# First pair of heads prepared on three engines, a new order of the attention, and a moved output and a moved turn in the expert stage

## The chip, the cores and the metric

One Trainium2 chip, one of its cores. The metric is the device time of one launch in microseconds (us). A core has five engines with their own instruction queues: PE (matrix multiplication, with its weight loads shown as PEld), DVE (vector), ACT (scalar), POOL (GpSimd) and SP, which here only issues transfers. An engine runs its queue in order.

## The reference, cut to what matters

Three steps, each on the result of the one before: attention with queries averaged in pairs, a dense layer pair with h − tanh(h), and a mixture of eight experts of which each token takes one.

```python
q_pool = q.reshape(B, H, S // 2, 2, D).mean(axis=3)        # B 2, H 8, S 1152, D 64
scores = scale * np.matmul(q_pool, k.transpose(0, 1, 3, 2))
attn = np.exp(scores - scores.max(-1)); attn /= attn.sum(-1) + 1e-9
x = (attn @ v) -> (1152, 512)
h = x @ w_in; x = (h - np.tanh(h)) @ w_out                  # 512 -> 2048 -> 512
logits = x @ w_gate; expert_idx = np.argmax(logits, axis=1) # 8 experts, 288 places each
y = relu(disp[e] @ w1[e]) @ w2[e]                           # 512 -> 1024 -> 512
out[i] = gate_w[i] * y[expert_idx[i], pos[i]]
```

## The kernel before

**Attention.** The 16 heads go in eight pairs. `load_k` (L513), `prep_q` (L547) and L596 load k, q and v of a pair through SP. To multiply in full precision, k and the summed q are split into a high and a low half: `khi` (L461) copies k rounded, `klo` (L470) subtracts it from k; `qadd` (L553) adds the two queries of a pair, `qhi` (twice) and `qlo` split the sum by the same helpers. All of these run on POOL. PE transposes them (`ktr` L534, `qtr` L570), and ACT moves the transposes out of PSUM (`kev`, `qev`, L459). Then a pair has nine units of 128 query rows: PE multiplies (`qk`, L664), DVE takes the maximum (L670), ACT the exponential (L678), POOL splits the result into two 16-bit halves (L689, two instructions a unit; ACT does a few of them, L691), and a transposing DMA from SP (L694) brings it into `pt`, a single buffer for all pairs. Units 3 and 7 of a pair are transposed on PE instead (L706, L720, L723). When the pair's units stand in `pt`, PE multiplies with v in two halves of 72 matmuls (L736; this is the AV phase), and only as its matmuls have read `pt` can the next pair's transposes write there. Behind it the sums are divided out (L800).

**Dense layers.** L906 multiplies with `w_in`, L963 with `w_out`; the weights are loaded during the attention and split by ACT and DVE (L873 to L880).

**Experts.** Rows are scattered to lists by expert; per expert one block of 64 rows always runs. `hidden(e)` (L1389) multiplies with w1, ACT applies relu (L1394), `turn(e)` transposes (four transposes on PE, L1400, into the one PSUM buffer `ht`, and one ACT copy into `hT`, L1404), `project(e)` (L1414, four chunks of w2) multiplies with w2, `output(e)` scales by the gate (ACT L1421, DVE L1424) and scatters to the result (POOL L1270). The gate values come with a small transfer of their own (L1332). The inputs of experts 0 and 1 stand transposed in PSUM first and are copied by `xth0` (L459 on ACT); those of the others are transposed by PE at L1349 and copied by `xth1` to `xth3` (L459 ACT, L460 DVE). Where an expert has more than 64 rows, the others run as its overflow: `over_first` transposes them (L1496), copies them on DVE (L1499), and multiplies with w1 (64 matmuls, L1503, relu on DVE L1506); a second half follows (L1518). With this data experts 0 and 4 have one.

**What sets the order.** A planner (class `Plan`) takes each operation with the buffers it reads and writes, a cost, and a due time `at` (shifted by kind through the table `ORDER`), and writes one order per engine: an operation goes in by due time once what it needs is there by the modelled times. In the expert stage `P.seq` keeps the order by due time alone:

```python
t = at + 9.9 if e == 0 else at + 5.0
over_first(e, t)
project(e, at + 5.6)
output(e, at + 9.2)
```

## Time and profile before

| what | before |
|---|---|
| median of 3 runs | 654.37 us (652.66 to 654.85) |
| the profiled execution | 655.12 us, span 653.1 us |
| TensorE's granted clock, mean | 0.971 |
| PE busy | 588.3 us (90%) |
| DVE, ACT, POOL busy | 373.9, 349.8, 348.0 us (57%, 54%, 53%) |

The span is the time from the first to the last instruction that the profile shows; the launch adds 2.0 us in this execution. Busy time is a sum over stages that have different limits, so a stage is read by itself: who is busy there, and for what the others wait. [...]

### The profile page before, as it was taken

What the parts mean: (1) busy time and instruction counts of PE and PEld (TensorE: products, weight loads), DVE (VectorE), ACT (ScalarE), POOL (GpSimd) and SP (SyncE); (2) the same over time, 40 slices, a digit from 0 to 9 for tenths busy, and PEclk for the clock granted to TensorE, in tenths of its full rate; (3) what the DMA queues carried; (4) which work ended last, traced back from release to release, by engine and by line L of the source; (5) the groups of instructions that cost most, each with busy time, mean ns of one, the idle gap of its engine ahead of it and who ended that gap; (6) DMA issues with size and microseconds to landing.
All of it is one profiled execution on the core that took longest, in us unless ns stands there. A gap on an engine that the chain in (4) does not pass through costs nothing. (4 is left out here: it accounts for less than half of the span.)

```text
span 653.1 us, 10491 instructions
## 1 busy us (share of the span) xinstructions
PE 588.3 (90%) x3840; PEld 471.9 (72%) x3840; DVE 373.9 (57%) x579; ACT 349.8 (54%) x641; POOL 348.0 (53%) x303
## 2 busy tenths in 40 slices
PE   3879898979898979999999999899999959999993
PEld 2767787867786868888899999799989456338331
DVE  1687767695777686898879896854554021101100
ACT  4886877776868786856775766544441100120011
POOL 7996959696969588976446365522232100110111
PEclk9979999998999999999999999899998979999997
DMA  7799989998999695999935123344277843595000
GB/s 217 167 200 204 218 195 204 219 212 172 192 214 211 128 176 124 162 349 356 411 131 178 34 67 95 119 139 129 67 215 249 224 128 129 178 371 190 22 24 13
DMA packets 172371, 114.82 MB, mean 176 GB/s; under 512 B 135470, under 2 KB 144686, under 8 KB 172048
## 3 DMA queue, kind: packets, MB, share of 16 engines
q1 hardware_dynamic: 169152, 109.37, 64.5%
q0 software_dynamic: 1680, 3.81, 1.9%
q10 hardware_dynamic: 1472, 0.79, 0.6%
q8 instruction: 37, 0.61, 0.4%
q14 instruction: 30, 0.25, 0.1%
HBM read 66.22 MB, written 16.15 MB: 126 GB/s over the span
## 5 line engine op out<-in xcount | busy, mean ns | idle before, releaser
L470 POOL TENSOR_TENSOR b<-b,b 128x512 fp32r<-128x512 f32 (+2 forms) x88 | 149.9, 1715 | 97.8 <-ACT b L459 80.6
L689 POOL TENSOR_SCALAR b<-b 128x1152 f16<-128x1152 uint16 (+1 forms) x110 | 131.5, 1216 | 42.1 <-ACT b L678 37.8
L963 PE MATMUL psum<-b,b 128*128 128x512 f32 x432 | 118.3, 400 | 4.3 <-POOL b L470 3.7
L670 DVE CUSTOM_DVE_ANT_1 b<-psum,na 128x1152 f16<-128x1152 f32 x72 | 97.5, 1355 | 42.5 <-PE psum L664 34.8
L906 PE MATMUL psum<-b,b 128*128 128x384 f32 x576 | 116.0, 340 | 1.0 <-DVE b L723 1.0
L906 PEld LDWEIGHTS psum<-b,b 128*128 128x128 f32 x576 | 103.8, 190 | 8.3 <-DVE b L723 1.3
L678 ACT ACTIVATE b<-psum,b 128x1152 int32<-128x1152 f32 (+1 forms) x72 | 88.0, 1222 | 39.3 <-DVE b L670 36.2
L664 PE MATMUL psum<-b,b 128*128 128x384 f32 x384 | 87.5, 365 | 18.0 <-ACT b L678 17.3
L963 PEld LDWEIGHTS psum<-b,b 128*128 128x128 f32 x432 | 79.5, 189 | 17.9 <-POOL b L470 5.4
L664 PEld LDWEIGHTS psum<-b,b 128*128 128x128 f32 x384 | 67.3, 197 | 26.6 <-ACT b L678 21.5
L459 ACT ACTIVATE b<-psum 128x384 fp32r<-128x384 f32 (+3 forms) x119 | 60.2, 540 | 46.1 <-PE psum L963 14.6
L736 PE MATMUL psum<-b,b 128*64 128x288 f16 x1152 | 81.1, 293 | 3.7 <-DMA b<-b 1.4
L736 PEld LDWEIGHTS <-b 128*64 128x64 f16 x1152 | 64.9, 112 | 15.7 <-issue 10.4
L459 ACT ACTIVATE b<-b 128x512 fp32r<-128x512 f32 (+1 forms) x56 | 39.7, 720 | 48.3 <-DVE b L937 25.8
L1270 POOL DMA_INDIRECT out_dram<-b,b x8 | 7.3, 916 | 80.2 <-DVE b L1424 40.2
L1424 DVE SCALAR_TENSOR_TENSOR b<-psum,b,b 64x512 f32<-64x512 f32 x8 | 5.9, 742 | 70.1 <-ACT b L1421 70.1
L1404 ACT ACTIVATE b<-psum 128x512 f32<-128x512 f32 x8 | 4.8, 597 | 58.6 <-PE psum L1400 58.6
L878 DVE SCALAR_TENSOR_TENSOR b<-b,b 128x512 uint32<-128x512 uint32 x32 | 34.7, 1101 | 0.2
L929 DVE SCALAR_TENSOR_TENSOR b<-psum,b 128x768 f32<-128x768 f32 x24 | 22.8, 952 | 17.3 <-ACT b L924 8.2
L880 DVE SCALAR_TENSOR_TENSOR b<-b,b 128x512 uint32<-128x512 uint32 x32 | 32.4, 1026 | 0.2
L1389 PE MATMUL psum<-b,b 128*64 128x512 f32 x128 | 30.6, 602 | 2.0 <-ACT b L459 1.4
L723 DVE SCALAR_TENSOR_TENSOR b<-psum,b 128x384 f16<-128x384 f32 x48 | 25.0, 551 | 12.1 <-ACT b L720 12.1
(130 smaller groups left out, 803.2 us busy)
## 6 DMA issues: line engine op xcount, KB each, us to landing
b<-in_moe_w_dram SPq DMA_DIRECT2D x64, 512.0 KB, 6.0
b<-in_moe_w_in_dram SPq DMA_DIRECT2D x32, 256.0 KB, 4.4
b<-in_moe_w_out_dram SPq DMA_DIRECT2D x16, 512.0 KB, 7.5
...
```

The source lines that it names most:

```text
L459: "a": ("act", (a_ps if ps else a_sb)(n), lambda: nc.scalar.activation(out=dst(), in_=src(), func=ACTF.Copy)),
L470: "p": ("pool", p2(n), lambda: nc.gpsimd.tensor_tensor(out=dst(), in0=a(), in1=b(), op=ALU.subtract)),
L664: nc.tensor.matmul(out=V(S_)[:, j, 0:CB], lhsT=lhsT, rhs=rhs[:, j * CB:(j + 1) * CB], start=(m == 0), stop=(m == len(mm) - 1))
L670: P.op([("dve", 1.43, lambda: nc.vector.tensor_tensor_reduce(out=V(junk), in0=V(S_)[:, :, 0:CB], in1=self.na[:, 3:4].unsqueeze(2).to_broad ...
L678: P.op([("act", 1.4, lambda: nc.scalar.activation(out=V(p).rearrange("p (a e) -> p a e", a=3), in_=V(S_)[:, :, 0:CB], func=ACTF.Exp, bias= ...
L689: P.op([("pool", p1(S), lambda a=a, src=src, by=by: nc.gpsimd.tensor_scalar(out=V(hl)[:, a], in0=src(), scalar1=by, scalar2=0.0, op0=ALU.m ...
L736: nc.tensor.matmul(out=V(ps)[i * D:(i + 1) * D, 0, 0:half], lhsT=V(v16[2 * c + i])[:, j, vl, :], rhs=V(pt)[:, hl * KT + j, i * SQ + g * ha ...
L878: (0.9, lambda: nc.vector.scalar_tensor_tensor(out=V(t), in0=lo(), scalar=29, in1=V(t), op0=ALU.logical_shift_right, op1=ALU.bitwise_or)),
L880: (0.9, lambda: nc.vector.scalar_tensor_tensor(out=V(t), in0=hi(), scalar=0x80000000, in1=V(t), op0=ALU.bitwise_and, op1=ALU.bitwise_or)),
L906: nc.tensor.matmul(out=V(h)[:, a, 0:384], lhsT=w, rhs=V(xx)[:, dk, sl], start=(n == 0), stop=(n == 11))
L963: nc.tensor.matmul(out=V(ps)[:, 0, :], lhsT=V(g[gi, blk, i][gl])[:, a, sl], rhs=V(wo[2 * gi + i, a])[:, wl, :], start=(i == 0 and a == 0 a ...
L1389: nc.tensor.matmul(out=V(h)[i * SM:(i + 1) * SM, 0, :], lhsT=V(xT[e // 2])[:, e % 2, k], rhs=V(w[e, k])[:, i * FH:(i + 1) * FH], start=(k ...
```

## The change

**First pair.** k of pair 0 is loaded as two transfers, a head each, and q as two transfers of five and four of its nine tiles. For head 0, `khi` goes to ACT and `klo` to DVE; for the first five tiles `qadd` and `qlo` go to DVE and `qhi` to ACT; the moves out of PSUM for the pair are shared by DVE and ACT. Head 1 and the last four tiles stay on POOL. **Order.** `ORDER` has new values throughout, and four settings of due times move a little; no operation is added by that. **Expert stage.** `xth0` is copied in two halves, by ACT and by DVE; `hT` gets two buffers; `output(0)` has a later due time than `over_first(0)`; the last `turn` has a due time inside `project(6)`.

```diff
-ORDER = {"av": -5.5, "c0": 12, "c1": 5, "c2": -6.5, "c3": -1.5, "cabs": -13.5, "kev": -2, "khi": -1.5, "klo": -6.5,
...
+ORDER = {"av": -4, "c0": 15.5, "c1": -5.5, "c2": -9.5, "c3": 0.5, "cabs": -14.5, "exp": 3, "h": 1.5, "kev": -2,
...
@@ -471,6 +471,14 @@
         }
         return [c[e] for e in engs]
 
+    def add_alts(self, dst, a, b, n, engs="vp"):
+        nc = self.nc
+        c = {
+            "v": ("dve", d1(n), lambda: nc.vector.tensor_tensor(out=dst(), in0=a(), in1=b(), op=ALU.add)),
+            "p": ("pool", p2(n), lambda: nc.gpsimd.tensor_tensor(out=dst(), in0=a(), in1=b(), op=ALU.add)),
+        }
+        return [c[e] for e in engs]
+
     def attention(self):
         nc, P = self.nc, self.P
         V = P.v
@@ -510,6 +518,12 @@
         def load_k(c, need):
             b, h = heads[2 * c]
             raw = kraw[c] = P.sb([2, KT, D], F32, f"kraw{c}")
+            if c == 0:
+                for i in range(2):
+                    P.op([("dma", 1.45, lambda i=i: nc.sync.dma_start(
+                        out=V(raw)[:, i].rearrange("p j d -> p (j d)"), in_=k[b, h + i].rearrange("(p j) d -> p (j d)", j=KT)))],
+                        w=[(raw, i)], at=need - CFG["kld"] + 3 * i, name=f"ldk{c}.{i}")
+                return
             P.op([("dma", 2.9, lambda: nc.sync.dma_start(
                 out=V(raw).rearrange("p i j d -> p i (j d)"), in_=k[b, h:h + 2].rearrange("i (p j) d -> p i (j d)", j=KT)))],
                 w=[raw], at=need - CFG["kld"], name=f"ldk{c}")
@@ -522,10 +536,11 @@
 
             sp = P.sb([KT, 2, D], F32R, f"ksp{n}")
             t = kT[n] = P.sb([S], F32R, f"kT{n}")
-            P.op(self.copy_alts(lambda: V(sp)[:, :, 0, :], rw, KT * D, CFG["khi"], slow=True), r=[raw], w=[(sp, 0)],
+            khi, klo, kev = ("a", "v", "va") if n == 0 else (CFG["khi"], CFG["klo"], CFG["kev"])
+            P.op(self.copy_alts(lambda: V(sp)[:, :, 0, :], rw, KT * D, khi, slow=True), r=[(raw, n % 2)], w=[(sp, 0)],
                  at=need - CFG["kpr"], name=f"khi{n}")
-            P.op(self.sub_alts(lambda: V(sp)[:, :, 1, :], rw, lambda: V(sp)[:, :, 0, :].bitcast(F32), KT * D, CFG["klo"]),
-                 r=[raw, (sp, 0)], w=[(sp, 1)], at=need - CFG["kpr"] + 1, name=f"klo{n}")
+            P.op(self.sub_alts(lambda: V(sp)[:, :, 1, :], rw, lambda: V(sp)[:, :, 0, :].bitcast(F32), KT * D, klo),
+                 r=[(raw, n % 2), (sp, 0)], w=[(sp, 1)], at=need - CFG["kpr"] + 1, name=f"klo{n}")
             for g in range(3):
                 ps = P.ps(1, F32R, f"kps{n}.{g}")
 
@@ -537,32 +552,41 @@
                 at = need - CFG["ktr"] + g
                 P.op([("pe", 3 * 0.115, pe_)], r=[sp], w=[ps], at=at, name=f"ktr{n}.{g}")
                 P.op(self.copy_alts(lambda g=g: V(t)[:, g * 384:(g + 1) * 384],
-                                    lambda ps=ps: V(ps)[:, 0, 0:384].bitcast(F32), 384, CFG["kev"], True),
+                                    lambda ps=ps: V(ps)[:, 0, 0:384].bitcast(F32), 384, kev, True),
                      r=[ps], w=[(t, g)], at=at + 0.3, name=f"kev{n}.{g}")
 
         def prep_q(c, need):
             raw = P.sb([NS, 2 * D], F32, f"qraw{c}")
 
             b, h = heads[2 * c]
-            P.op([("dma", 2.9, lambda: nc.sync.dma_start(
-                out=V(raw), in_=q[b, h:h + 2].rearrange("i (s r) d -> (i s) (r d)", r=2).rearrange("(t p) e -> p t e", p=128)))],
-                w=[raw], at=need - CFG["qld"], name=f"ldq{c}")
             s = P.sb([NS, D], F32, f"qs{c}")
             t = P.sb([NS, 3, D], F32R, f"qsp{c}")
-            n = NS * D
-            P.op(CFG["sel"]("qadd", [("pool", p2(n), lambda: nc.gpsimd.tensor_tensor(out=V(s), in0=V(raw)[:, :, 0:D], in1=V(raw)[:, :, D:2 * D], op=ALU.add)),
-                  ("dve", d1(n), lambda: nc.vector.tensor_tensor(out=V(s), in0=V(raw)[:, :, 0:D], in1=V(raw)[:, :, D:2 * D], op=ALU.add))]),
-                 r=[raw], w=[s], at=need - CFG["qpr"], name=f"qadd{c}")
-            for j in (0, 2):
-                P.op(self.copy_alts(lambda j=j: V(t)[:, :, j, :], lambda: V(s), n, CFG["qhi"], slow=True), r=[s], w=[(t, j)],
-                     at=need - CFG["qpr"] + 1, name=f"qhi{c}.{j}")
-            P.op(self.sub_alts(lambda: V(t)[:, :, 1, :], lambda: V(s), lambda: V(t)[:, :, 0, :].bitcast(F32), n, CFG["qlo"]),
-                 r=[s, (t, 0)], w=[(t, 1)], at=need - CFG["qpr"] + 2, name=f"qlo{c}")
+            first = c == 0
+            for pt, (t0, t1) in enumerate(((0, NF + 1), (NF + 1, NS)) if first else ((0, NS),)):
+                key = pt if first else None
+                n = (t1 - t0) * D
+                at = need - CFG["qpr"] + 2 * pt
+                early = first and pt == 0
+                qadd, qhi, qlo = ("v", "a", "v") if early else (CFG["qadd"], CFG["qhi"], CFG["qlo"])
+                P.op([("dma", 2.9 * (t1 - t0) / NS, lambda t0=t0, t1=t1: nc.sync.dma_start(
+                    out=V(raw)[:, t0:t1],
+                    in_=q[b, h:h + 2].rearrange("i (s r) d -> (i s) (r d)", r=2).rearrange("(t p) e -> p t e", p=128)[:, t0:t1]))],
+                    w=[(raw, key)], at=need - (CFG["kld"] - 1 - 4 * pt if first else CFG["qld"]), name=f"ldq{c}.{pt}" if first else f"ldq{c}")
+                P.op(self.add_alts(lambda t0=t0, t1=t1: V(s)[:, t0:t1], lambda t0=t0, t1=t1: V(raw)[:, t0:t1, 0:D],
+                                   lambda t0=t0, t1=t1: V(raw)[:, t0:t1, D:2 * D], n, qadd),
+                     r=[(raw, key)], w=[(s, key)], at=at, name=f"qadd{c}.{pt}" if first else f"qadd{c}")
+                for j in (0, 2):
+                    P.op(self.copy_alts(lambda t0=t0, t1=t1, j=j: V(t)[:, t0:t1, j, :], lambda t0=t0, t1=t1: V(s)[:, t0:t1], n, qhi,
+                                        slow=True), r=[(s, key)], w=[(t, (key, j))], at=at + 1, name=f"qhi{c}.{j}")
+                P.op(self.sub_alts(lambda t0=t0, t1=t1: V(t)[:, t0:t1, 1, :], lambda t0=t0, t1=t1: V(s)[:, t0:t1],
+                                   lambda t0=t0, t1=t1: V(t)[:, t0:t1, 0, :].bitcast(F32), n, qlo),
+                     r=[(s, key), (t, (key, 0))], w=[(t, (key, 1))], at=at + 2, name=f"qlo{c}")
             qt = qT[c] = P.sb([2, 2 * NF, 128], F32R, f"qT{c}")
             zt = qT[c, "z"] = self.zb[c % 2]
             groups = [(0, 0), (1, 0), "z", (0, 1), (1, 1)]
             for gi, g in enumerate(groups):
                 ps = P.ps(1, F32R, f"qps{c}.{gi}")
+                tr = [(t, (int(gi > 2) if first else None, j)) for j in range(3)]
                 blocks = [(g[0], s_ + g[1] * (NF + 1)) for s_ in range(NF)] if g != "z" else [(0, NF), (1, NF)]
 
                 def pe_(ps=ps, blocks=blocks):
@@ -571,10 +595,10 @@
                                             in_=V(t)[:, s_, hl:hl + 2, :].rearrange("p a d -> p (a d)"), identity=ident_r)
 
                 at = need - CFG["qtr"] + gi
-                P.op([("pe", len(blocks) * 0.105, pe_)], r=[t], w=[ps], at=at, name=f"qtr{c}.{gi}")
+                P.op([("pe", len(blocks) * 0.105, pe_)], r=tr, w=[ps], at=at, name=f"qtr{c}.{gi}")
                 if g != "z":
                     P.op(self.copy_alts(lambda g=g: V(qt)[:, g[0], g[1] * NF:(g[1] + 1) * NF, :].rearrange("p a e -> p (a e)"),
-                                        lambda ps=ps: V(ps)[:, 0, :].bitcast(F32), 512, CFG["qev"], True),
+                                        lambda ps=ps: V(ps)[:, 0, :].bitcast(F32), 512, "va" if first else CFG["qev"], True),
                          r=[ps], w=[(qt, g)], at=at + 0.3, name=f"qev{c}.{gi}")
                 else:
                     def zev(eng, ps=ps):
@@ -1298,7 +1322,7 @@
 
         P.op([("all", 2.5, vals)], r=[self.cnt_tok, self.xs_tok], at=T2 - CFG["vat"], name="vals")
 
-        P.limit = low = P.spaces["sb"].size - 10 * 4096
+        P.limit = low = P.spaces["sb"].size - 10 * 4096 - 2048
 
         def static(shape, dtype, name):
             nonlocal low
@@ -1312,7 +1336,7 @@
         xbs = [static([2, 514], F32, f"xb{i}") for i in range(3)]
         xT = [static([2, DK, SM], F32, f"xT{j}") for j in range(E // 2)]
         hs = [static([FH], F32, "hs")] * 2
-        hT = [static([FC, 2, SM], F32, "hT")] * 2
+        hT = [static([FC, 2, SM], F32, f"hT{i}") for i in range(2)]
         yo = [static([512], F32, f"yo{i}") for i in range(2)]
         hp = [P.ps(1, None, f"hp{i}") for i in range(2)]
         ht, yp, ov = P.ps(1, None, "ht"), P.ps(1, None, "yp"), P.ps(4, None, "ov", top=True)
@@ -1359,6 +1383,11 @@
             if j:
                 P.op([("pe", DK * 0.11, trx)], r=[(ho, 1)], w=[(ov, j)], at=at, name=f"xtr{j}")
             eng = "av"[j % 2]
+            if j == 0:
+                for i in range(2):
+                    P.op(self.copy_alts(lambda i=i: V(xT[0])[:, i], lambda i=i: V(ov)[:, :, i * SM:(i + 1) * SM], 256, "av"[i], True),
+                         r=src, w=[(xT[0], i)], at=at + 0.02, name=f"xth0.{i}")
+                continue
             P.op(self.copy_alts(lambda j=j: V(xT[j]), xpv, 512, eng, True), r=src, w=[xT[j]], at=at + 0.02, name=f"xth{j}")
 
         rel, w, used = {}, {}, [0]
@@ -1389,7 +1418,7 @@
                         nc.tensor.matmul(out=V(h)[i * SM:(i + 1) * SM, 0, :], lhsT=V(xT[e // 2])[:, e % 2, k],
                                          rhs=V(w[e, k])[:, i * FH:(i + 1) * FH], start=(k == 0), stop=(k == DK - 1))
 
-                P.op([("pe", 0.87, mm)], r=[xT[e // 2], w[e, k]], w=[h], at=at + 0.87 * (k - lo), name=f"h{e}.{k}")
+                P.op([("pe", 0.87, mm)], r=[(xT[0], e) if e < 2 else xT[e // 2], w[e, k]], w=[h], at=at + 0.87 * (k - lo), name=f"h{e}.{k}")
             if hi == DK:
                 P.op([("act", a_ps(512), lambda: nc.scalar.activation(out=V(hs[e % 2]), in_=V(h)[:, 0, :], func=ACTF.Relu))],
                      r=[h], w=[hs[e % 2]], at=at + 0.87 * (hi - lo) + 0.1, name=f"hs{e}")
@@ -1462,13 +1491,13 @@
             x0 = xbs[e % 3]
             if e + 1 < E:
                 hidden(e + 1, at + 0.7, 0, 2)
-            turn(e, at + 2.5)
+            turn(e, at - EP + 5.6 + 0.87 * 2.5 if e == E - 1 else at + 2.5)
             if e + 1 < E:
                 hidden(e + 1, at + 3.0, 2, DK)
             t = at + 9.9 if e == 0 else at + 5.0
             over_first(e, t)
             project(e, at + 5.6)
-            output(e, at + 9.2)
+            output(e, at + (9.95 if e == 0 else 9.2))
             t = at + EP + 2.4 if e == 0 else at + 9.3
             over(e, 1, t)
             over_on("z", "dve", e, t + 0.1, [(ov, 2), (ov, 3)], [x0])
@@ -1548,7 +1577,7 @@
            sel=sel, zat=40, t2=12, ep=10, vat=1, eld=40, xld=4.0,
            rts=([6, 7, 8],), ovc=(10.5, 0.5, 0.5, 0.5), vhi='a',
            rd='a', xf='v', qadd='p', tu=3.4, t0=20, kld=32, kpr=14, ktr=11, qld=28, qpr=13, qtr=9, vld=14, vpr=5,
-           avg=2.7, av0=10.5, avs=2.0, fin=11.5, t1=21, hp=8.1, wld=8, wcv=20, wsp=17, cv0=60, cvs=25, fn0=2, hch=6, xadd='ppvppvppv', xof=6,
+           avg=2.7, av0=9.5, avs=3, fin=12, t1=21, hp=8.1, wld=8, wcv=20, wsp=17, cv0=55, cvs=25, fn0=2, hch=6, xadd='ppvppvppv', xof=6,
            pena=(2.0, 2.0), khi='p', klo='p', kev='a', qhi='p', qlo='p', qev='a', ave='a',
            xhi='p', xlo='p', whi='a', wlo='p', ghi='a', glo='p', xe0='a')
 
```

On POOL at the start of the kernel, before: `khi` for both heads, `klo`, `qadd` (L553) and the split of q for pair 0; then the same for pair 1, of which only the last three instructions are shown; then the first halves of the exponentials (L689).

```order
L461 TENSOR_SCALAR b_115<-b_111 128x9x64
L461 TENSOR_SCALAR b_117<-b_111 128x9x64
L470 TENSOR_TENSOR b_115<-b_111,b_115 128x9x64
L553 TENSOR_TENSOR b_122<-b_113 128x576
L470 TENSOR_TENSOR b_117<-b_111,b_117 128x9x64
L461 TENSOR_SCALAR b_143<-b_122 128x9x64 x2
L470 TENSOR_TENSOR b_143<-b_122,b_143 128x9x64
...
L461 TENSOR_SCALAR b_231<-b_198 128x9x64 x2
L470 TENSOR_TENSOR b_231<-b_198,b_231 128x9x64
L689 TENSOR_SCALAR b_261<-b_241 128x1152 x2
L689 TENSOR_SCALAR b_285<-b_264 128x1152 x2
```

And what stands there in the changed kernel (its lines are some 24 higher: L478 is the addition, L713 the halves):

```order
L461 TENSOR_SCALAR b_143<-b_111 128x9x64
L470 TENSOR_TENSOR b_143<-b_111,b_143 128x9x64
L478 TENSOR_TENSOR b_128<-b_113 128x256
L461 TENSOR_SCALAR b_133<-b_128 128x4x64 x2
L470 TENSOR_TENSOR b_133<-b_128,b_133 128x4x64
L713 TENSOR_SCALAR b_202<-b_186 128x1152 x2
L713 TENSOR_SCALAR b_221<-b_200 128x1152 x2
L478 TENSOR_TENSOR b_241<-b_204 128x576
L713 TENSOR_SCALAR b_252<-b_233 128x1152 x2
L461 TENSOR_SCALAR b_280<-b_241 128x9x64 x2
```

The full-size `klo`, `qadd`, `qhi` and `qlo` of head 0 and the first tiles are gone from the queue, a quarter-size addition and split are left, and the preparation of pair 1 stands behind the first halves of the exponentials and no longer ahead of them.

On DVE at the first overflow, before (b_5643 is the output of expert 0, the two copies at L460 are `xth1` and `xth3`, L1499 and L1506 belong to `over_first(0)`):

```order
L1482 UNCONDITIONAL_BRANCH x2
L1424 SCALAR_TENSOR_TENSOR b_5643<-psum,b_5590,b_5643 64x512
L460 COPY b_5656<-psum 128x512
L460 COPY b_5661<-psum 128x512
L1492 COMPARE_AND_BRANCH
L1499 COPY b_5663<-psum 128x448 x2
L1506 TENSOR_SCALAR b_5583<-psum 128x2x224 x4
L1492 UNCONDITIONAL_BRANCH x2
```

And in the changed kernel, where L1453 is the output, L1528 and L1535 are the overflow's:

```order
L460 COPY b_5652<-psum 128x512
L460 COPY b_5660<-psum 128x512
L1521 COMPARE_AND_BRANCH
L1528 COPY b_5662<-psum 128x448 x2
L1535 TENSOR_SCALAR b_5589<-psum 128x2x224 x4
L1521 UNCONDITIONAL_BRANCH x2
L1453 SCALAR_TENSOR_TENSOR b_5712<-psum,b_5595,b_5712 64x512
L1543 COMPARE_AND_BRANCH
```

The output's instruction has moved from ahead of the two copies to behind the overflow's four relus. On ACT and POOL the output's other two instructions move with it.

On PE near the end, before: the four chunks of `project(6)`, the last turn, and the first chunks of `project(7)` (rows of overflow code that isn't run are left out):

```order
L1414 MATMUL psum<-b_6145,b_5626 64x512 x2
L1414 MATMUL psum<-b_6147,b_5626 64x512 x2
L1414 MATMUL psum<-b_6149,b_5626 64x512 x2
L1414 MATMUL psum<-b_6157,b_5626 64x512 x2
...
L1400 MATMUL psum<-ident,b_5616 128x128 x4
...
L1414 MATMUL psum<-b_6180,b_5626 64x512 x2
L1414 MATMUL psum<-b_6185,b_5626 64x512 x2
```

And in the changed kernel (L1443 is `project`, L1429 the turn):

```order
L1443 MATMUL psum<-b_6153,b_5631 64x512 x2
L1443 MATMUL psum<-b_6155,b_5631 64x512 x2
L1443 MATMUL psum<-b_6161,b_5631 64x512 x2
L1429 MATMUL psum<-ident,b_5619 128x128 x4
L1443 MATMUL psum<-b_6185,b_5631 64x512 x2
...
L1443 MATMUL psum<-b_6191,b_5756 64x512 x2
L1443 MATMUL psum<-b_6193,b_5756 64x512 x2
```

The four transposes have moved from behind the fourth chunk of `project(6)` to between its third and its fourth.

## Rows read from the trace of the kernel before

**Rows 1.** The page of the profile, its first line.

```profile
span 653.1 us, 10491 instructions
```

**Rows 2.** Windows: busy time of each engine, TensorE's granted clock, DMA share.

```profile
core 0: us, PE busy (x) PEld busy (x) DVE busy (x) ACT busy (x) POOL busy (x), PEclk, DMA share, GB/s
0.00:17.10 17.10, 6.40 (x37) 5.02 (x38) 2.72 (x12) 7.04 (x16) 13.67 (x38) 1.00 0.72 208
17.10:51.40 34.30, 27.99 (x158) 24.86 (x157) 27.78 (x43) 28.57 (x58) 33.25 (x29) 0.90 0.90 191
51.40:83.50 32.10, 27.91 (x259) 23.08 (x259) 23.11 (x42) 23.49 (x47) 25.32 (x23) 1.00 1.01 209
229.19:261.50 32.31, 28.98 (x263) 24.31 (x263) 23.25 (x42) 24.24 (x48) 26.45 (x23) 1.00 0.81 146
286.50:500.00 213.50, 208.93 (x1075) 187.25 (x1075) 154.69 (x200) 118.70 (x188) 98.73 (x58) 0.99 0.51 173
```

**Rows 3.** Timeline, the start of the attention: start, duration, engine, line, operation, [idle before it <-releaser].

```profile
5.59 1.31 POOL L461 TENSOR_SCALAR b<-b 128x576 fp32r<-128x576 f32 x2 [2.46 <-DMA b<-in_k_dram]
...
8.31 1.00 PE L534 MATMUL psum<-ident_r,b 128*128 128x128 f32 x6 [8.31 <-POOL b L470]
...
13.80 1.23 PE L570 MATMUL psum<-ident_r,b 128*128 128x128 f32 x8
...
17.10 2.25 PE L664 MATMUL psum<-b,b 128*128 128x384 f32 x6
...
19.50 1.36 DVE L670 CUSTOM_DVE_ANT_1 b<-psum,na 128x1152 f16<-128x1152 f32 x1 [3.17 <-PE psum L664]
...
21.52 1.20 ACT L678 ACTIVATE b<-psum,b 128x1152 int32<-128x1152 f32 x1
```

**Rows 4.** Timeline of the same stretch: DVE operations with two SBUF inputs, and POOL.

```profile
20.56 1.45 POOL L470 TENSOR_TENSOR b<-b,b 128x576 fp32r<-128x576 f32 x1
...
20.98 1.65 DVE L642 SCALAR_TENSOR_TENSOR b<-b,b,b 128x576 f16<-128x576 f32 x1
...
23.83 0.82 DVE L642 SCALAR_TENSOR_TENSOR b<-b,b,b 128x576 f16<-128x576 f32 x1
```

**Rows 5.** Timeline of PE: the first and the last of the eight AV phases.

```profile
51.44 1.66 PE L736 MATMUL psum<-b,b 128*64 128x288 f16 x24
...
276.30 0.93 PE L736 MATMUL psum<-b,b 128*64 128x288 f16 x12
```

**Rows 6.** Timeline, the first overflow of the expert stage.

```profile
523.57 1.50 PE L1349 MATMUL psum<-ident,b 128*128 128x128 f32 x12 [1.01 <-DMA b<-xs]
...
529.00 0.69 ACT L1421 ACTIVATE b<-psum,b 64x512 f32<-64x512 f32 x1 [9.17 <-DMA b<-xs]
...
529.72 0.74 DVE L1424 SCALAR_TENSOR_TENSOR b<-psum,b,b 64x512 f32<-64x512 f32 x1 [24.11 <-ACT b L1421]
530.39 1.27 DVE L460 COPY b<-psum 128x512 f32<-128x512 f32 x2
...
531.12 1.01 PE L1496 MATMUL psum<-ident,b 112*128 112x112 f32 x4 [5.66 <-DVE b L460]
...
532.34 14.45 PE L1503 MATMUL psum<-b,b 128*128 128x224 f32 x64 [0.21 <-DVE b L1499]
```

**Rows 7.** Windows and PE's timeline: the clock there, and the second overflow.

```profile
530.00:535.00 5.00, 3.67 (x11) 3.15 (x12) 2.79 (x5) 0.31 (x1) 0.96 (x1) 0.50 0.13 30
...
591.63 12.37 PE L1503 MATMUL psum<-b,b 128*128 128x224 f32 x64 [0.33 <-DVE b L1499]
```

**Rows 8.** Timeline, the last turn of the expert stage.

```profile
634.64 3.65 PE L1414 MATMUL psum<-b,b 128*64 128x512 f32 x16 [0.31 <-PEq L1492]
...
638.45 0.63 PE L1400 MATMUL psum<-ident,b 128*128 128x128 f32 x4
...
639.17 0.60 ACT L1404 ACTIVATE b<-psum 128x512 f32<-128x512 f32 x1 [0.15 <-PE psum L1400]
...
639.89 3.65 PE L1414 MATMUL psum<-b,b 128*64 128x512 f32 x16 [0.82 <-DVEq L1525]
```

More of the change, by code (lines that the diff above doesn't have):

```diff
@@ L155, in cost @@
     return d
[L158 to L162 removed]
+ORDER = {"av": -4, "c0": 15.5, "c1": -5.5, "c2": -9.5, "c3": 0.5, "cabs": -14.5, "exp": 3, "h": 1.5, "kev": -2,
+         "khi": 5, "klo": -9.5, "ktr": -1, "l": -2.5, "ldk": 1, "ldq": 1.5, "ldv": 1.5, "ldw": -6, "pth": 4.5,
+         "ptl": 4.5, "qadd": -3.5, "qev": 18.5, "qhi": 10, "qk": -2.5, "qlo": -8, "qtr": 11.5, "rbe": -5, "rbt": -1.5,
+         "rbz": -1, "rd": 7.5, "rec": -3, "rze": -6, "sv": 13.5, "tr": 13.5, "vbc": 3.5, "vlo": 9.5, "vsc": -5.5,
+         "vsum": -5.5, "vtr": 6, "xf": -6.5, "xhi": 13, "xlo": -1}
 def kind(name):
```

4 lines of the change are left out of this document (removed).

## The prediction

> **What bounds the kernel now.** I read the windows by stage first, then the timelines of the places that the change touches. The span is 653.1 us [rows 1]; the profiled execution took 655.12, so 2.0 us lie around it, and it stands 0.75 us above the median of 654.37. The sum below is made against 655.1 and then lowered by 0.75.
>
> The stages have different limits. In the first 17.1 us PE works 6.40 us and POOL 13.67: PE waits for its first operands. From there to the first AV phase POOL works 33.25 of 34.30 us [rows 2], so POOL sets when the units of pair 0 are ready. Then eight AV phases follow, from 51.44 to 276.30 [rows 5], which is 224.9 us for seven loops, 32.1 a loop. PE works 27.91 of 32.10 us in the first of these and 28.98 of 32.31 in a late one [rows 2]; no engine is full. The loop is the chain "AV phase has read `pt`, transposes of the next pair write it, next AV phase". Its length does not depend on when it began, so time won ahead of 51.44 should move all eight phases. Behind it PE works 208.93 of 213.50 us [rows 2]: nothing there can swallow or give back much. The expert stage is PE's too, with one large hole, which the change aims at.
>
> **The change part by part. A, the first pair.** Before, POOL starts on k when both heads have landed, at 5.59; head 0 can be transposed at 8.31, behind two copies and a subtraction; q's transposes come at 13.80, the first product at 17.10, its maximum ends at 19.50 + 1.36 = 20.9, the first exponential starts at 21.52 [rows 3]. After, by the same rows:
> - half of k lands earlier by the time that 288 KB take; at the stage's 208 GB/s [rows 2] that is 1.4 us, bounds 0 and 1.4. I take 1.0: 4.6.
> - `khi` on ACT: 0.60 us for 512 elements [rows 8], times 576/512 = 0.68, so 5.3. `klo` on DVE is an operation with two SBUF inputs. It took 0.82 once and 1.65 once, the latter while POOL ran a subtraction from 20.56 [rows 4]. Here POOL's first instruction needs head 1, which lands later, so 0.82: 6.1.
> - nine transposes at 1.00/6 = 1.5: 7.6. The moves out of PSUM end at about 8.1.
> - q's five tiles: by then landed; `qadd` 5/9 of 0.82 = 0.46, `qhi` twice 0.60 x 320/512 = 0.75 in all, both beside k's transposes; `qlo` behind DVE's move, 0.46: 8.6. Transposes 1.23 [rows 3]: 9.8; move 0.60: 10.4.
> - product and maximum took 20.9 − 17.1 = 3.8 us together: exponential at 14.2. PE's six matmuls of 2.25 us [rows 3] are its first full ones; were they quicker, up to 1 us less. I take 13.6, with 13.1 and 15.8 (all of k late, all three DVE operations at the double price) as bounds. That is 7.9 us earlier.
>
> From the first exponential to the sixth transposed unit POOL then has 19 instructions where it had 18, since part of pair 1's preparation now stands behind the copies, less one copy that ACT does: one more at 33.25/29 = 1.15 us [rows 2]. Sum of A: −7.9 + 1.1 = **−6.8**, bounds −4.6 and −10.6. The far bound takes the clock in: it is 0.90 over 34.30 us [rows 2], so 3.4 us are lost to it; another order may be without that, or keep it, and I count nothing.
>
> [...]
>
> **B, the overflow.** PE's transposes at 523.57 wait 1.01 us for the rows' transfer and take 1.50; then it stands still 5.66 us, until DVE's copies. These are queued behind the output's DVE instruction (529.72), and that behind ACT's, which waited 9.17 us for the gate values and started at 529.00 [rows 6]. With the output moved, DVE copies `xth1` as soon as its transposes are out and `xth3` at the end, 523.57 + 1.50 = 525.1, for 1.27/2 = 0.64: 525.7. Then the second transposes (1.01 at the low clock, about half at the high one) and one more copy follow; before, 531.12 to 532.34 was 1.2 us, so L1503 starts at 526.6 to 526.9. I take 526.7: **−5.6**, bounds −5.9 and, if some other copy takes the place, −3. The moved output now waits behind the four relus. It costs nothing: the next user of its PSUM is `project(1)`, with the rest of the overflow and part of `hidden(2)` ahead of it; without that cover ACT's 0.69 and DVE's 0.74 would show. Next late is the transfer for which PE waits 1.01 at 523.57.
>
> The hole also cost clock. From 530 to 535 the granted clock is 0.50, the lower of its two levels, right behind PE's stillness, and the 64 matmuls take 14.45 us; expert 4's, behind 0.33 us of idleness, take 12.37 [rows 6, 7]. With the hole at about 1 us I count the whole difference, **−2.1**, bounds 0 and −2.1.
>
> **C, the rest.** `xth0` in halves lets PE start some 0.3 us earlier; but the 1.01 us of waiting for the transfer [rows 6] swallows it: 0. It would be worth −0.3 if that transfer started earlier too. The last turn: `project(6)` ends at 634.64 + 3.65 = 638.29 and `project(7)` begins at 639.89, a gap of 1.60 [rows 8]. After, the transposes' 0.63 still cost PE time, with some 0.3 for getting in and out; ACT's copy (0.60, and 0.1 on each side) lies beside the fourth chunk, 3.65/4 = 0.91. Saved: 1.60 − 0.93 = **−0.6**, bounds −0.3 and −0.9. The second `hT` only makes this possible. Without it the copy would wait for that chunk. The new `ORDER` shuffles seven loops that have 4 us of free PE time each; the trace of before cannot show what it does. I count 0, bounds ±4.
>
> Sum: −6.8 − 5.6 − 2.1 − 0.6 = −15.1; 655.1 − 15.1 = 640.0, and 0.75 less, 639.2.
>
> **The rivals.** *R1, the transfers bound the loops.* Their DMA share is 1.01 in the first loop; ahead of 51.4 it is 0.72 and 0.90 [rows 2]. The idle share there is 17.1 x 0.28 + 34.3 x 0.10 = 8.2 us, of which the first 4 or 5 us can't be used before data has come. Were the engines of the DMA the limit, only about 3 us of A could be kept: 639.2 + 3.8 = 643.0. Against it: a late loop with a share of 0.81 is as long, 32.31 us.
>
> *R2, the other sign: the new order lengthens the loop.* A unit's transposing DMA needs both copied halves. Where one of these is now on ACT, it queues behind exponentials, and the AV phase waits for the last. To eat the 15.1 us, each of seven loops has to grow by 2.2 us, and then 654.4 is reached; at 3 us a loop it is about 660. For it speaks that PE's free 4.2 us show slack that a worse order can fill; against it, that only five such copies in all are on ACT, where two were, and that the amount of work per loop is unchanged.
>
> *R3, prices at their upper bound.* DVE pays the double price for all three operations (+1.7), or the low clock stays in the overflow (+2.1), or both: 640.9 to 643.0.
>
> *R4, the new order shortens the loops or is without the low clock ahead of 51.4* (3.4 us): 632 to 636.
>
> *R5, no change:* A is lost to the order's side effects and the hole is only moved to another wait, 653 to 656.
>
> **How the numbers follow.** Forecast (636.5 to 642) 0.50, R1 0.14, R3 0.10, R4 0.13, R2 0.08 (0.06 of it past the point), R5 0.05. About 0.3% (2 us) is what a measurement of this kernel can tell from no change. Faster by more: 0.89; within 0.3%: 0.04; slower: 0.07. The range 632 to 648 leaves out R5, R2 and a part of R4.
>
> **What would show it.** A: the first exponential near 13.6 and the first AV phase near 44.6, both in the timeline; loops of 32.1 us. A first AV phase near 44 with longer loops is R1 if the DMA share is at 1 in them, R2 if PE or SP wait for copies on ACT. B: PE idle for at most 1 us ahead of the second L1496, and the 64 matmuls in about 12.4 us at a clock of 1.00. C: the last two projections 0.95 us apart. I am wrong if the loops change by over half a microsecond each, or if the hole comes back behind another instruction.

## The result and the profile after

The changed kernel takes 645.53 us (median of 3 runs, 644.52 to 646.90) against 654.37: ratio 0.9873, 95% interval 0.9832 to 0.9913. That is 8.8 us faster, inside the range; 639.2 was forecast. The profiled execution's span is 642.7 us where it was 653.1 [rows 1].

**The start of the attention**, against [rows 3], in the timeline of the changed kernel:

```profile
4.54 0.68 ACT L459 ACTIVATE b<-b 128x576 fp32r<-128x576 f32 x1 [2.47 <-DMA b<-in_k_dram]
5.26 0.76 DVE L469 TENSOR_TENSOR b<-b,b 128x576 fp32r<-128x576 f32 x1 [2.34 <-ACT b L459]
...
6.07 1.00 PE L549 MATMUL psum<-ident_r,b 128*128 128x128 f32 x6 [6.07 <-DVE b L469]
...
7.21 0.48 DVE L477 TENSOR_TENSOR b<-b 128x320 f32<-128x320 f32 x1
...
8.48 0.59 DVE L469 TENSOR_TENSOR b<-b,b 128x320 fp32r<-128x320 f32 x1
...
9.13 1.26 PE L594 MATMUL psum<-ident_r,b 128*128 128x128 f32 x8 [1.16 <-DVE b L469]
...
10.96 4.17 PE L688 MATMUL psum<-b,b 128*128 128x384 f32 x12
...
13.35 1.36 DVE L694 CUSTOM_DVE_ANT_1 b<-psum,na 128x1152 f16<-128x1152 f32 x1 [1.59 <-POOL b L470]
...
14.75 1.23 ACT L702 ACTIVATE b<-psum,b 128x1152 int32<-128x1152 f32 x1 [3.72 <-DVE b L694]
```

The steps came nearly as priced: `khi` 0.68, `klo` 0.76, `qadd` 0.48, `qlo` 0.59, none at the double price (1.65 for 0.82 in [rows 4]). k's transposes and moves take turns and end 0.5 us later than assumed, and product and maximum again take 3.75 us (10.96 to 14.71), so the first exponential starts at 14.75 and not at 13.6: 6.77 us earlier than before. But the first AV phase does not follow it. In the timeline of PE (starts of the AV phases of pairs 0, 1, 2 and 7), against [rows 5]:

```profile
51.95 1.29 PE L760 MATMUL psum<-b,b 128*64 128x288 f16 x10
...
82.37 1.66 PE L760 MATMUL psum<-b,b 128*64 128x288 f16 x24
...
111.85 1.35 PE L760 MATMUL psum<-b,b 128*64 128x288 f16 x13 [0.99 <-DVE b L747]
...
272.37 7.54 PE L760 MATMUL psum<-b,b 128*64 128x288 f16 x120
```

The second and the third phase before:

```profile
83.55 3.20 PE L736 MATMUL psum<-b,b 128*64 128x288 f16 x48 [0.96 <-ACT b L678]
...
114.90 1.73 PE L736 MATMUL psum<-b,b 128*64 128x288 f16 x24 [0.67 <-ACT b L459]
```

The first phase starts at 51.95 where it was 51.44. From the second on PE is ahead: by 1.2 us there, 3.1 at the third and 3.9 at the last. Two windows of the stretch from the first exponential to the first AV phase, with the columns of [rows 2], and ahead of them the same stretch of the kernel before:

```profile
21.52:51.44 29.92, 23.61 (x145) 20.90 (x144) 25.91 (x41) 26.25 (x54) 28.83 (x25) 0.89 0.94 190
```

```profile
14.75:51.95 37.20, 28.95 (x157) 25.03 (x155) 27.07 (x46) 32.90 (x68) 35.64 (x32) 0.83 0.96 198
45.00:52.00 7.00, 5.90 (x25) 5.16 (x27) 6.28 (x8) 5.64 (x13) 7.00 (x7) 0.50 1.00 217
```

POOL is busy in 35.64 of 37.20 us with 32 instructions; before, it had 25 there, for 28.83 us. The DMA engines are at 0.96, and the granted clock is at 0.50 from 45 to 52. (The clock is a share, 1.00 the most that a window shows. In steps of 0.25 us through the kernel before it is 1.00 in 2455, 0.50 in 144 and between the two in 13, all of these at an end of one of seven stretches at 0.50; these are the two levels of which the prediction speaks.) PE also has 84 products (`qk` matmuls in the program's order) ahead of the AV phase, where it had 78.

**The expert stage**, against [rows 6]: the rows' transfer is issued at 503.30, PE's transposes of them wait for it, ACT's part of the output stands behind `xth2`, and the 64 matmuls follow.

```profile
503.30 1.32 ACTq L1352 DMA_DIRECT2D b<-xs  x2
...
518.07 2.79 PE L1373 MATMUL psum<-ident,b 128*128 128x128 f32 x12 [4.47 <-DMA b<-xs]
...
520.67 0.69 ACT L1450 ACTIVATE b<-psum,b 64x512 f32<-64x512 f32 x1
...
522.42 13.14 PE L1532 MATMUL psum<-b,b 128*128 128x224 f32 x64
```

The stall that the change aimed at (5.66 us) is gone. Another stands ahead of it: 4.47 us at L1373, where before 1.01 us were waited. The matmuls still take 13.14 us. The windows show why:

```profile
495.00:500.00 5.00, 5.00 (x47) 5.00 (x45) 1.62 (x11) 0.00 (x0) 2.58 (x3) 1.00 1.03 411
515.00:520.00 5.00, 1.93 (x9) 1.96 (x10) 0.69 (x1) 0.00 (x0) 0.00 (x0) 0.72 0.40 80
520.00:525.00 5.00, 4.94 (x23) 4.47 (x22) 1.94 (x3) 1.28 (x2) 0.00 (x0) 0.60 0.00 0
```

Ahead of the rows' transfer the DMA engines move 411 GB/s, and what SP issues there are weight loads. PE stands from 513.60 to 518.07, and while it stands the clock falls: in steps of 0.25 us it is 1.00 up to 517.0 and 0.50 from 517.25 to 524.0, which makes the means of 0.72 and 0.60.

**The last turn**, against [rows 8]:

```profile
623.52 2.79 PE L1443 MATMUL psum<-b,b 128*64 128x512 f32 x12 [0.31 <-PEq L1521]
...
626.25 0.66 PE L1429 MATMUL psum<-ident,b 128*128 128x128 f32 x4
626.83 1.08 PE L1443 MATMUL psum<-b,b 128*64 128x512 f32 x4
...
629.47 3.65 PE L1443 MATMUL psum<-b,b 128*64 128x512 f32 x16 [1.56 <-DVEq L1554]
```

The four transposes are inside `project(6)` now, and PE still stands 1.56 us ahead of `project(7)`: from 626.83 + 1.08 to 629.47. Before, the whole gap was 1.60 with the transposes in it, so it got no shorter: from the start of `project(6)` to that of `project(7)` it was 5.25 us (634.64 to 639.89) and is 5.95 now (623.52 to 629.47).

A table by stage, from the starts of `hidden(0)` in the timelines (the expert stage is the rest of the span):

| kernel | hidden(0) starts | expert stage |
|---|---|---|
| before | 511.31 | 141.8 |
| changed | 502.34 | 140.4 |

So the first part gained 9.0 us in these two executions and the expert stage 1.4, where 6.8 and 8.3 had been forecast.

### The profile page after: what moved, and what is told of

Read it like the earlier page. It is cut to its first block, busy times and chain, and to the rows that moved or that the text cites. A ratio compares the mean times of both kernels' runs of the same rounds, so it can differ in the third digit from the quotient of the medians.

```text
span 642.7 us, 10537 instructions
## 1 busy us (share of the span) xinstructions
PE 583.7 (91%) x3840; PEld 467.5 (73%) x3840; DVE 388.6 (60%) x596; ACT 349.9 (54%) x634; POOL 336.2 (52%) x298
## 5 line engine op out<-in xcount | busy, mean ns | idle before, releaser
L470 POOL TENSOR_TENSOR b<-b,b 128x576 fp32r<-128x576 f32 (+2 forms) x87 | 141.2, 1633 | 103.3 <-ACT b L459 68.7
L713 POOL TENSOR_SCALAR b<-b 128x1152 f16<-128x1152 int16 (+1 forms) x107 | 127.5, 1213 | 39.0 <-ACT b L702 29.4
L702 ACT ACTIVATE b<-psum,b 128x1152 int32<-128x1152 f32 (+1 forms) x72 | 88.0, 1223 | 32.1 <-DVE b L694 23.6
L688 PE MATMUL psum<-b,b 128*128 128x384 f32 x384 | 87.4, 366 | 12.5 <-ACT b L702 12.4
L459 ACT ACTIVATE b<-psum 128x384 fp32r<-128x384 f32 (+4 forms) x114 | 58.2, 534 | 47.1 <-PE psum L987 13.3
L688 PEld LDWEIGHTS psum<-b,b 128*128 128x128 f32 x384 | 68.1, 198 | 16.4 <-ACT b L702 15.1
L760 PEld LDWEIGHTS <-b 128*64 128x64 f16 x1152 | 62.6, 110 | 16.1 <-issue 10.5
L459 ACT ACTIVATE b<-b 128x512 fp32r<-128x512 f32 (+3 forms) x59 | 40.8, 710 | 47.0 <-DVE b L961 29.3
L1006 DVE TENSOR_TENSOR b<-b,b 128x512 f32<-128x512 f32 x14 | 22.6, 1613 | 22.1 <-ACT b L459 22.1
L1453 DVE SCALAR_TENSOR_TENSOR b<-psum,b,b 64x512 f32<-64x512 f32 x8 | 5.9, 742 | 46.8 <-ACT b L1450 46.8
L904 DVE SCALAR_TENSOR_TENSOR b<-b,b 128x512 uint32<-128x512 uint32 x32 | 33.7, 1069 | 0.1
L1418 PE MATMUL psum<-b,b 128*64 128x512 f32 x128 | 30.6, 602 | 2.1 <-DMA b<-in_moe_w_dram 1.5
L1443 PE MATMUL psum<-b,b 128*64 128x512 f32 x128 | 29.4, 597 | 3.2 <-PEq L1521 1.6
L958 DVE SCALAR_TENSOR_TENSOR b<-b,b 128x768 f32<-128x768 f32 x24 | 28.9, 1206 | 4.6 <-ACT b L951 3.2
```

The source lines that it names most:

```text
L459: "a": ("act", (a_ps if ps else a_sb)(n), lambda: nc.scalar.activation(out=dst(), in_=src(), func=ACTF.Copy)),
L470: "p": ("pool", p2(n), lambda: nc.gpsimd.tensor_tensor(out=dst(), in0=a(), in1=b(), op=ALU.subtract)),
L688: nc.tensor.matmul(out=V(S_)[:, j, 0:CB], lhsT=lhsT, rhs=rhs[:, j * CB:(j + 1) * CB], start=(m == 0), stop=(m == len(mm) - 1))
L702: P.op([("act", 1.4, lambda: nc.scalar.activation(out=V(p).rearrange("p (a e) -> p a e", a=3), in_=V(S_)[:, :, 0:CB], func=ACTF.Exp, bias= ...
L713: P.op([("pool", p1(S), lambda a=a, src=src, by=by: nc.gpsimd.tensor_scalar(out=V(hl)[:, a], in0=src(), scalar1=by, scalar2=0.0, op0=ALU.m ...
L760: nc.tensor.matmul(out=V(ps)[i * D:(i + 1) * D, 0, 0:half], lhsT=V(v16[2 * c + i])[:, j, vl, :], rhs=V(pt)[:, hl * KT + j, i * SQ + g * ha ...
```

## The experiments

All ratios are to the kernel before, run beside it on the same chip, with 95% intervals. Not all experiments ran on the same chip; where two ran together, the text says so.

**x_expert: the edits of the expert stage alone.**

```diff
-            output(e, at + 9.2)
+            output(e, at + (9.95 if e == 0 else 9.2))
... (xth0 in halves, two hT, the last turn: as in the change)
```

> The kernel before with the edits of the expert stage alone (later output, turn inside the projection, halved first copy, two hT). If the mechanism of part B holds and only the changed kernel's early arrival at the stage spoils it (the transfer of the rows then collides with weight loads), it is 7 to 8 us faster, the second L1496 waits under 1 us and the 64 matmuls take about 12.4. If the rows' transfer is what comes late whenever the output is moved, it is only 2 to 3 us faster. The moved turn is worth 0 in both if the projection waits for its single PSUM buffer yp (0.6 by the prediction).

643.98 us, ratio 0.9869 (0.9825 to 0.9913): 8.9 us faster. The timeline:

```profile
527.20 1.53 PE L1349 MATMUL psum<-ident,b 128*128 128x128 f32 x12
...
530.13 12.35 PE L1508 MATMUL psum<-b,b 128*128 128x224 f32 x64 [0.64 <-DVE b L1504]
```

No wait for the rows is shown, and the matmuls take 12.35. The expert stage lasts 133.4 us (hidden(0) at 516.01, span 649.4; the six executions took 641.6 to 651.6 us, and this one 651.56). The mechanism of part B holds, and is worth 8.4 us when the rows are on time. Against this stage that of the changed kernel is 7.0 us longer: the wait of 4.47 is 4.5 of them, the slower transposes (2.79 for 1.53) 1.3 and the slower matmuls (13.14 for 12.35) 0.8.

**x_split and x_order: the first pair's split alone, and the order table alone.** The first takes the parts of the diff from `add_alts` to `qtr`, the second `ORDER` and the four settings:

```diff
+            khi, klo, kev = ("a", "v", "va") if n == 0 else (CFG["khi"], CFG["klo"], CFG["kev"])
...
-           avg=2.7, av0=10.5, avs=2.0, fin=11.5, ...
+           avg=2.7, av0=9.5, avs=3, fin=12, ...
```

> The kernel before with the split of the first pair alone, old order table. By the prediction's part A 6.8 us faster with the first AV phase near 44.6. If the lead is lost because the transposing DMAs of pair 0 are slowed by a full DMA load, the first exponential comes 6 to 8 us earlier but the first AV phase stays within 2 us of 51.4 and the time moves by 0 to 2 us. If it is the new order table that loses the lead (pair 1's products ahead of the first AV phase on PE), this run keeps 5 us or more of it.

> The kernel before with the new order table and the four settings alone. By the prediction's part C 0. If the 9 us by which the changed kernel reaches the expert stage earlier come from the order (shorter loops of pairs 1 and 2, fewer waits for POOL and one low-clock stretch less in the dense layers), it is 5 to 9 us faster. If they come from the split, it is within 2 us of before or slower.

The split alone: 669.74 us, 1.0269 (1.0239 to 1.0298), 17 us slower. The order alone: 656.82 us, 1.0059 (1.0030 to 1.0087), 4 us slower. Neither outcome of either expectation was that. In x_order's expert stage PE has both waits, for the rows and, the output standing at its old place, for DVE's copies (us in all, times, longest):

```profile
PE psum L1349 <- DMA b<-xs: 3.8, 1, 3.8
PE psum L1496 <- DVE b L460: 3.1, 1, 3.1
```

In x_split the first exponential starts at 14.63, and yet the first AV phase at 55.6. The wait of PE there (in the same columns), and DVE's and POOL's timelines of the stretch ahead of it:

```profile
PE psum L760 <- ACT b L702: 7.2, 1, 7.2
```

```profile
44.95 7.94 DVE L666 SCALAR_TENSOR_TENSOR b<-b,b,b 128x576 f16<-128x576 f32 x1
52.81 0.20 DVE L773 RECIPROCAL b<-b 128x9 f32<-128x9 f32 x1
```

```profile
44.61 1.42 POOL L478 TENSOR_TENSOR b<-b 128x576 f32<-128x576 f32 x1
...
50.87 1.41 POOL L470 TENSOR_TENSOR b<-b,b 128x576 fp32r<-128x576 f32 x1
55.67 1.37 POOL L713 TENSOR_SCALAR b<-b 128x1152 f16<-128x1152 uint16 x1 [3.39 <-ACT b L702]
```

PE waits 7.2 us for ACT, which waits for DVE, and DVE spends 7.94 us in one operation that elsewhere in this trace takes 0.76 at least and 1.20 in the median. It ends 0.6 us after POOL, busy with seven instructions from 44.61 to 52.28 without a gap, stops.

**x_vlo1: the same with one SBUF input in that operation.** The low half of v is v itself here, so the output is another.

```diff
-   nc.vector.scalar_tensor_tensor(out=V(t)[:, :, 1, :], in0=V(raw)[:, i], scalar=..., in1=V(t)[:, :, 0, :], ...)
+   nc.vector.tensor_reduce(out=V(t)[:, :, 1, :], in_=V(raw)[:, i].unsqueeze(3), axis=AX.X, op=ALU.max)
```

> The split alone (as x_split), with the low half of v made by a DVE operation with one SBUF input in place of one with two; the low half is then v itself, so the output is another. In x_split one such DVE operation took 7.94 us, as long as POOL ran without a gap, and the first AV phase waited 7.2 us. If the two inputs are the cause, no such operation takes over 1.5 us here, the wait ahead of the first AV phase is gone and the time is 5 to 9 us under x_split. If the split alone is slow for its order, it stays within 3 us of x_split.

664.00 us, 1.0181 (1.0138 to 1.0224): 5.7 us less than x_split. The first AV phase starts at 48.7 for 55.6, PE's wait for ACT there is 1.5 us for 7.2, and the 16 operations take 0.69 to 0.75 us. So the operation of 7.94 us cost about what its row says; all 16 were exchanged, so this is not shown for that one alone. The rest of x_split's loss has no cause shown. A part of it lies in the loops: from the fourth to the fifth AV phase x_split takes 37 us (157.4 to 194.5), where a loop of the kernel before takes 32.1, and x_vlo1 takes 39.

**x_split_order: both, without the expert stage's edits.**

> The changed kernel without the edits of the expert stage: split and new order table together. Alone the split took 17 us more and the order 4 us more than before. If the two only work together (the order was made for the split), this run is 4 to 8 us faster than before and reaches the expert stage 6 to 9 us earlier; the edits of the expert stage then add only 1 to 4 us on top of it, where alone they were worth 8.9. If the parts simply add, it is about 20 us slower; if attention and dense layers gain nothing, it equals before and the expert edits are the whole gain.

646.76 us, 0.9920 (0.9892 to 0.9947): 5.5 us faster. Split and order belong together; 17 and 4 us slower alone, they are faster as a pair. hidden(0) starts at 503.07, and the waits on PE from there on begin with these (us in all, times, longest):

```profile
PE psum L1373 <- DMA b<-xs: 5.1, 1, 5.1
PE psum L1413 <- DMA b<-in_moe_w_dram: 1.4, 1, 1.4
```

5.1 us for the rows; the wait ahead of the overflow's second transposes, 5.66 before, is not in the list, though the output stands at its old place. Behind this wait of 5.1 us the gate values no longer came last. The expert stage takes 140.1 us: with its edits, in the changed kernel, 140.4.

**x_yp7 and x_tail: the last projection.** The first writes it to another PSUM bank, the second also puts the skipped overflow parts of experts 6 and 7 behind it:

```diff
+        def ypo(e):
+            return hp[0] if e == E - 1 else yp
...
-            t = at + 9.9 if e == 0 else at + 5.0
+            t = at + 9.9 if e == 0 else at + 9.6 if e == E - 1 else at + 5.0
...
-            t = at + EP + 2.4 if e == 0 else at + 9.3
+            t = at + EP + 2.4 if e == 0 else at + EP + 9.25 if e == E - 2 else at + 9.9 if e == E - 1 else at + 9.3
```

> The changed kernel with the last projection written to the PSUM bank of hidden(6), which is free by then, and no longer to the one that output(6) still reads. If the last projection waits for that bank (1.56 us of PE idle in the changed kernel's trace), it is 1.2 us faster than the changed kernel and that wait is gone. If it waits for the turn's copy, as the prediction had it, nothing changes.

> The changed kernel with the last projection in the bank of hidden(6) and with the skipped overflow parts of experts 6 and 7 (branches only, with this data) behind the last projection on every engine. If the gap of 1.56 us ahead of the last projection is PE's walk through these branches, it shrinks to about 0.3 and the time by 1.2 us (about what can be measured). If it is the turn's copy or the PSUM bank, the gap stays.

x_yp7: 644.23 us, 0.9868 (0.9840 to 0.9896), as the changed kernel. The projection still waits:

```profile
632.28 3.65 PE L1446 MATMUL psum<-b,b 128*64 128x512 f32 x16 [1.45 <-PEq L1524]
```

x_tail: 645.81 us, 0.9892 (0.9849 to 0.9935). There the gap is gone, `project(7)` follows as part of one group, but from the last scatter to the end of the span (645.8) it takes 9.25 us, in the changed kernel 634.91 to 642.7, 7.8:

```profile
630.26 4.51 PE L1446 MATMUL psum<-b,b 128*64 128x512 f32 x20
...
636.55 0.91 POOL L1294 DMA_INDIRECT out_dram<-b,b  x1 [2.52 <-DVEq L1557]
```

The gap is thus PE's walk through branches that skip the overflow code, but for the 0.1 us that the other bank took from it in x_yp7 (1.45 for 1.56); moved behind, it is paid at the end, 1.5 us there.

**x_late, x_late16: the changed kernel with the weight loads from the 29th (17th) chunk on held back** until the rows have landed:

```diff
+        gate = static([16], F32, "gate")
+        P.op([("dma", 0.1, lambda: nc.sync.dma_start(out=V(gate)[:, 0:8], in_=xe()[:, E // 2 - 1, DM - 8:DM]))],
+             r=[(ho, 1)], w=[gate], at=T2 + 4, name="gate")
...
-            P.op([("dma", 1.47, ld)], r=[(ovt, gr)], w=[c],
+            P.op([("dma", 1.47, ld)], r=[(ovt, gr)] + ([gate] if n >= 28 else []), w=[c],
```

> The changed kernel with the expert weights from the 29th chunk on held back on SP until the rows for experts 2 to 7 have landed (a tiny transfer that reads them stands ahead on the queue). If these weight loads slow the rows' transfer (PE waits 4.47 us for it in the changed kernel, 0 to 1 us elsewhere), that wait falls under 1.5 us and the kernel is 3 to 5 us faster than the changed one. If the transfer is late for its own issue, nothing changes; if the held weights come too late for their experts, it is slower.

> The changed kernel with the weights held back from the 17th chunk on and not from the 29th. The rows were on time already with the 29th, so no gain is left: within 2 us of 640.7. Slower by more if the weights of experts 2 and 3 then come too late.

640.67 us, 0.9820 (0.9779 to 0.9860), and 640.64 us, 0.9860 (0.9801 to 0.9918): some 5 us under the changed kernel's median, by the ratios to before 3.5 and 0.9. The intervals overlap with the change's own, since the runs of before scatter; but the six runs of x_late (638.9 to 641.7) all lie under the three of the changed kernel, and under all six of x_tail (642.2 to 647.5) beside it on the same chip. Its profile shows where from:

```profile
505.41 5.37 PE L1421 MATMUL psum<-b,b 128*64 128x512 f32 x24 [1.35 <-ACT b L459]
...
516.60 1.53 PE L1373 MATMUL psum<-ident,b 128*128 128x128 f32 x12
...
519.53 12.35 PE L1535 MATMUL psum<-b,b 128*128 128x224 f32 x64 [0.64 <-DVE b L1531]
```

```profile
497.00:502.00 5.00, 5.00 (x49) 4.93 (x48) 2.22 (x15) 0.00 (x0) 1.67 (x2) 1.00 0.22 84
```

The wait for the rows is gone, the matmuls take 12.35, and ahead of the stage the DMA engines are at 0.22 with 84 GB/s, where the changed kernel had 1.03 with 411.

**x_expert_late, x_so_late, x_before_late: the held loads with the expert stage's edits alone, with split and order alone, and with nothing else.**

> A control: the kernel before with the edits of the expert stage and the held weight loads. There PE did not wait for the rows, so if the held loads help by keeping the rows on time alone, they change nothing here (within 2 us of 644.0). If they help in another way (weights later, less memory traffic in general), it is 3 to 5 us faster.

> Split, new order and the held weight loads, without the edits of the expert stage. With the rows on time the gate values should again be what comes last, so PE waits for DVE's copies behind the output (5.66 us in the kernel before) and the clock falls behind that wait. Then this run is within 2 us of split and order alone (646.8), and the edits of the expert stage are worth 6 to 8 us beside the held loads (640.7 with them). If the held loads alone make the gain, it is 641 to 643.

> The kernel before with the held weight loads alone: no edit of the change. If the slow transfers of gate values and rows beside the weight loads are the common cause of the stillness in the expert stage, then ACT no longer waits for the gate values, the wait of 5.66 us ahead of the overflow's second transposes falls under 1 us, the 64 matmuls take about 12.4 us, and the run is 7 to 9 us faster than before, as fast as the edits of the expert stage alone (8.9). If moving the output is needed in the old order, it is 0 to 3 us.

x_expert_late: 643.34 us, 0.9900 (0.9855 to 0.9945), as x_expert: the control holds. x_so_late: 639.92 us, 0.9846 (0.9791 to 0.9901). My expectation fell: the stall at the output does not come back.

```profile
515.75 0.69 ACT L1448 ACTIVATE b<-psum,b 64x512 f32<-64x512 f32 x1 [2.78 <-PE psum L1441]
...
517.86 0.39 PEld L1523 LDWEIGHTS psum<-ident,b 112*128 112x128 f32 x4 [0.53 <-DVE b L460]
...
519.08 12.35 PE L1530 MATMUL psum<-b,b 128*128 128x224 f32 x64 [0.62 <-DVE b L1526]
```

ACT's part of the output starts as soon as `project(0)` has ended; the gate values are there already. x_before_late: 642.06 us, 0.9830 (0.9788 to 0.9872), 11.4 us under the 653.49 of before beside it, without any edit of the change: as much as the whole change gives, if not more (640.9 to 644.1 in six runs, against 644.5 to 646.9; the ratios' intervals overlap). 8.4 us of it lie in the expert stage; that hidden(0) starts 3.9 us earlier in this execution (507.39) the held loads don't explain. Issue and landing of the gate values, 4 KB, in the kernel before and here:

```profile
L1332 ACTq DMA_DIRECT2D b<-xs x2: 724/932/1139, 511.8 to 513.0; - x2
...
DMA to landing us min/median/max: 15.8/15.8/15.8
```

```profile
L1332 ACTq DMA_DIRECT2D b<-xs x2: 622/685/748, 507.9 to 508.5; - x2
...
DMA to landing us min/median/max: 6.6/6.8/7.1
```

15.8 us from issue to landing before, 6.8 with the weight loads out of the way. ACT issues the rows' two transfers, 384 KB each, right ahead of these; they take 11.3 us before and 6.1 here. PE's waits in x_before_late from 490 on begin with:

```profile
PE psum L1417 <- PEq L1495: 1.7, 5, 0.4
PE psum L1392 <- ACT b L459: 1.4, 1, 1.4
```

Neither the rows' transfer nor the gate's is in that list any more. The expert stage lasts 133.4 us in x_before_late, 133.3 in x_so_late, 133.7 in x_late, 133.5 in x_expert_late: whatever the output's place. With the rows on time the edits of the expert stage gain 0.5 us from hidden(0) to the 64 matmuls (14.1 for 14.6) and lose 0.7 at the last turn (5.95 for 5.25, as in the changed kernel).

## Why the prediction was right, and where its sum was not

- **Direction and range** held, but the number came about by two misses against each other: ahead of the expert stage the two executions differ by 9.0 us for a forecast of 6.8, and in it by 1.4 for 8.3. The sum was −15.1 us; the two halves measured −5.5 (A and C's order) and −8.9 (the expert stage's edits) alone, −14.4 if they added up, but together they gave 8.8. Two of the prediction's own signs of being wrong came: the hole is back behind another instruction, and the seven loops shrank by 0.6 us each (51.95 to 272.37, 31.5 a loop for 32.1). The step that failed is in part B: "Next late is the transfer for which PE waits 1.01 at 523.57". I named it and left it at 1.01. In the kernels with split and new order it is 4.47 to 5.1 us, with the new order alone 3.8, with the split alone 1.8, and in x_split_order it alone has replaced the stall that B removes. So it grows with the order table, which the prediction had at 0. The cause is shown from both sides: with the weight loads held back the wait is gone in the changed kernel, and in the kernel before the stall goes without moving the output. Both waits were for transfers issued by ACT beside 512 KB loads from SP: the rows (two of 384 KB) and behind them the gate values (4 KB). The growth of the wait has two halves. Against the start of hidden(0) the rows' transfer is issued 1.85 us later (0.96 behind it at 503.30; before, 510.42, 0.89 ahead), and from issue to PE's start it takes 14.77 us for 13.15. That makes the 3.46 us by which 4.47 exceeds 1.01. SP issues its last six weight loads between 495.5 and 505.3, thus around that issue; but before, eight were issued from 494.7 to 512.9, around the rows' issue too. Why the wait is longer in the new order is open.
- **A, the first exponential:** 6.77 us earlier for 7.9, the steps as priced. **A, the first AV phase** near 44.6: wrong, 51.95. The term that failed is "one more" POOL instruction at 1.15 us: between first exponential and first AV phase POOL ran seven more (32 for 25), 6.8 us of work, as much as the lead. Work that it no longer did first came later. That POOL alone ate the lead is not shown, for 84 products with a stretch at a clock of 0.50 also stand ahead on PE. The gain came another way: in the seven traces with the changed attention hidden(0) starts between 502.3 and 505.7, mean 504.3; in the four with the old one between 507.4 and 516.0, mean 510.7, and 508.9 without x_expert's long execution. That is 4.6 to 6.4 us for a forecast of 6.8. Medians of runs taken together on one chip, with the rows on time, give less: 643.34 with the old attention (x_expert_late), 639.92 with the new (x_so_late), 3.4 us. In the two profiled executions 3.9 us are won up to the last AV phase and 5.0 between it and hidden(0), where by the prediction nothing could "give back much"; PE's waits for POOL fell there from 3.7 to 1.2 us, and the rest is unexplained. I don't call the mechanism of A right for that.
- **C, the order table** at 0 with ±4: as an addend it does not exist. Alone it costs 4, the split alone 17, together they gain 5.5.
- **B, the clock:** the 64 matmuls take 12.34 or 12.35 us in x_expert and the five traces with held loads, where the longest wait for rows or copies ahead of them is 0.64 us (forecast 12.4), 13.01 to 13.18 in x_tail, the changed kernel and x_split_order, where PE waits 4.47 to 5.1 us for the rows alone, and 13.89 in x_vlo1 and 14.45 before, where it waits 7.2 and 5.66 us for DVE's copies, too. In the changed kernel that is −1.3 us of the −2.1. **C, xth0:** 0 as forecast. **C, the turn:** −0.6 forecast; the stretch got 0.7 us longer. I took the gap for ACT's copy, and it is PE's walk through branches (x_tail).
- **R1:** the DMA engines did decide, but not in the loops: at the entry of the expert stage, where the rows came late while the engines were at 1.03 with weight loads. **R2** did not happen in the changed kernel; x_split, the split under the old order, shows that it can go so: there PE waits 7.2 us for ACT. **R3:** no double price in the three operations named; its other half, the low clock in the overflow, came in part (0.50 up to 524.0, 13.14 us for the matmuls). **R5:** its second half came, the hole moved to another wait.
